# Batch 0 of a linear-attention and MLP kernel: x of two tiles made transposed and centred by TensorE, with w1 and w2 loaded in other parts

## The chip, the cores and the metric

The kernel runs on one core of a Trainium2 chip. The metric is the device time of one execution in microseconds, as the median of repeated runs. Profiles come from one profiled execution; their times count from the start of the program's span.

## The reference

```python
# batch 8, heads 8, seq 576, head_dim 64; all float32
q_s = exp(q - max) / sum          # softmax over head_dim
k_s = exp(k - max) / sum          # softmax over seq
kv  = einsum('bhsd,bhse->bhde', k_s, v)
att = einsum('bhsd,bhde->bhse', q_s, kv)
x   = att.transpose(0, 2, 1, 3).reshape(8, 576, 512)
mu, var = mean(x, -1), mean((x - mu) ** 2, -1)
xn  = (x - mu) / sqrt(var + 1e-6) * g_ln
out = x + maximum(xn @ w_ch1, 0) @ w_ch2      # 512 -> 2048 -> 512
```

## The kernel before

The 576 rows of a batch are split into 512 rows, which make a chunk of four tiles of 128, and 64 left over; the leftovers of all eight batches make a ninth chunk. The MLP of chunk 0 uses plain products. From chunk 1 on its second product, and from chunk 2 on its first product too, is done with seven block products instead of eight, from sums of blocks that VectorE and GpSimd prepare.

**Order of work.** Nothing is scheduled by a planner. `run(mlp_steps(c), side)` goes through the list of the MLP's matmuls on TensorE (PE). Each has a weight: 1 for an mm2 of 512 columns, 0.5 for 256 columns, 0.25 for 128. A side entry `(position, function)` is emitted ahead of the first matmul whose weights summed so far reach the position. In chunk 0 the first product (`mm1_part`) fills weights 0 to 64 and the second (`mm2_stream`) 64 to 128. Each engine executes its instructions in the order in which they were emitted. PE, VectorE (DVE), ScalarE (ACT), GpSimd (POOL) and the sync engine (SP) all have such an order.

**PSUM.** There are eight banks: two in the pool `att_ps` (tag `a`), six in `mm_ps` (tag `m`). A new tile of a tag takes the buffer that was taken longest ago, and waits until that one has been read.

**Start.** `first_batch` (it ends where the first `run` begins) emits batch 0 before any MLP work:
- SP loads q's first half (tiles 0 and 1) and k in four parts. POOL loads v in three parts, q's rest (tiles 2 and 3), then w1 and w2 with conversion to bf16.
- `warm(n)` is n matmuls on a tile of zeros, which nobody reads.
- `exp_qt`, `norm_q`: exp of q on ACT, then row sums, reciprocal and multiply on DVE. `eq_pT` transposes a tile by four PE transposes and copies it to `eqT`.
- `exp_k0` on ACT, `z0_mm` (column sums by PE), `recip_z`, then `kv0_mm`: 18 small matmuls for each of four pairs of heads, two pairs in one PSUM tile, and four DVE multiplies into `kv_sb`, whose blocks are diagonal.
- Tiles 0 and 1: `po_half` multiplies eqT by kv in two halves and ACT copies each half to x with a running sum; `sum_halves` adds the two sums; `xn_out` subtracts the mean on DVE; for tile 0 two pairs of PE transposes follow, each brought out by DVE with a multiply by the gain (`g_col`, the gain over 512) into `xnT`.
- Tile 1's transposes (`xn_pT`) and all of tiles 2 and 3 (`q0_rest`: sums of eqT by PE and the product; `x_fast`: scaling, sum and centring on DVE) are side entries of chunk 0.

The variance is not needed until the end of the MLP: the row's rstd scales the second product's result.

**Chunk 0's first product** takes tile 0 and tile 1 apart for the first four blocks of 128 output rows (m), 128 columns to a matmul, then both tiles together for m 4 to 7, then tiles 2 and 3 apart for m 0 to 3:

```python
parts = ((0, 2, 0, 1), (0, 2, 1, 1), (2, 2, 0, 1), (2, 2, 1, 1), (4, 4, 0, 2), (0, 4, 2, 1),
         (0, 4, 3, 1), (4, 4, 2, 2), (8, 4, 0, 2), (8, 4, 2, 2), (12, 4, 0, 2), (12, 4, 2, 2))
```

An entry is (first m, how many, first tile, how many tiles), with four contraction steps (ko) each.

**Later.** Chunk 1's attention is emitted in chunk 0's second product: `kv_all(1)` needs the leftover rows of k and v (`prep_kvrem`), which POOL loads after w1, w2, q and k.

Of the kernel before, what the change touches and what calls it, by code (L numbers as in the profile page):

```python
# [12 lines left out]
FP32 = mybir.dt.float32  # L13
# [7 lines left out]
def kernel(  # L21
# [52 lines left out]
    scrap = const.tile([P, 512], BF16)  # L74
    bones = const.tile([P, 2], BF16)
    w1_sb = wts.tile([P, KO1, DH], BF16, tag="w1", name="w1_raw")
    w1g = const.tile([P, KO1, DH], BF16)
    g_col = const.tile([P, KO1], FP32)
    ident_f = const.tile([KO1, KO1], FP32)
# [14 lines left out]
    def load_w2(g4):  # L94
        rows = slice(4 * g4, 4 * g4 + 4)
        nc.gpsimd.dma_start(w2_sb[:, rows, :], w2_src[:, rows, :])
# [187 lines left out]
    def kv0_mm(j):  # L284

        if j % 2 == 0:
            kvbox["p0"] = att_ps.tile([P, 2, 256], FP32, tag="a", name="pkv")
        pkv = kvbox["p0"]
        for t in range(T0):
            for ps in halves:  # L290
                nc.tensor.matmul(
                    pkv[ps, j % 2, 0:D], eks[0][ps, j, t], raws["v0"][ps, j, t],
                    start=(t == 0), stop=(t == T0 - 1),
                )
        if j % 2:
            for ps in halves:
                nc.vector.tensor_mul(
                    kv_sb[ps, 0, j - 1 : j + 1, ps], pkv[ps, :, 0:D],
                    kvbox["rz"][ps, j - 1 : j + 1].to_broadcast([64, 2, D]),
                )  # L300
# [45 lines left out]
    def po_mm(c, t, i):  # L346


        if i == 0:
            pool, tag = (mm_ps, "m") if c == 0 and t >= 2 else (att_ps, "a")  # L350
            pobox["p"] = pobox[c, t] = pool.tile([P, DM], FP32, tag=tag, name="po")
# [39 lines left out]
    def po_half(t, half):  # L391

        pool, tag = (mm_ps, "m") if half else (att_ps, "a")
        po = pool.tile([P, DM], FP32, tag=tag, name="po")
        for i in range(2):
            j = 2 * half + i
            nc.tensor.matmul(
                po[:, i * P : i * P + P], eqTs[0][:, t, j, :], kv_sb[:, 0, j, :],
                start=True, stop=True,
            )  # L400
        x, st, _, _ = xs[0]
        nc.scalar.activation(
            x[:, t, DH2 * half : DH2 * half + DH2], po[:, 0:DH2], AF.Copy,
            accum_out=st[:, t, half : half + 1],
        )

    def sum_halves(t):
        _, st, _, mv = xs[0]
        nc.vector.tensor_add(mv[:, t, 0:1], st[:, t, 0:1], st[:, t, 1:2])
# [120 lines left out]
    def prod(n, bank, t, k, first=False, own=False):  # L530

        at = slice(t * P, t * P + P)
        if n in (1, 2, 4):
            odd, half = ((0, 0), (1, 0), None, (1, 1))[n - 1]
            lhsT = hbox["h"][:, 2 * k + odd, 2 * half + t, :]
        else:
            lhsT = hbox["s"][:, {5: 0, 6: 1, 7: 2, 3: 3}[n], k, at]
        if n in (1, 2):
            rhs = w2_sb[:, 2 * k + n - 1, 0:DH2]
        elif n == 3:  # L540
            rhs = w2_sb[:, 2 * k + 1, DH2:DM]
        else:
            rhs = w2_q[:, {5: 0, 6: 1, 7: 2, 4: 3}[n], k]
        nc.tensor.matmul(hbox[bank][:, t], lhsT, rhs, start=first and (own or t == 0) and k == 0,  # L544
                         stop=k == KH - 1, skip_group_check=True)
# [28 lines left out]
    def last_products(product):  # L574
# [6 lines left out]

        def stt(t, col, src, add=None):
# [17 lines left out]
        def own_bank():  # L600
            bank("d")

        def seed_e():
# [15 lines left out]
        product(4, "d", ts=(1,), own=True, at={  # L619
            15: [lambda: stt(3, 0, hbox["d"][:, 1], part(3, 0)), lambda: store(3, 1, 0)]})  # L620

    def mm2_fast(c):
# [3 lines left out]
        def product(n, name, first=False, at=None, ts=range(2), own=False, cut=None):  # L626
            at = at or {}
            order = [(t, k) for t in ts for k in range(KH)]
            if cut:
                order = [(t, k) for ks in (range(cut), range(cut, KH)) for t in ts for k in ks]  # L630
            for i, (t, k) in enumerate(order):

                def go(t=t, k=k, i=i):
                    if i == 0 and first:
                        bank(name)
                    prod(n, name, t, k, first or own, own)
                    for fn in at.get(i + KH * ts[0], []):
                        fn()

                steps.append((0.5, go))  # L640
# [104 lines left out]
    def mlp_steps(c):  # L745
# [4 lines left out]
        if c == 0:  # L750
            full = range(0)
            parts = ((0, 2, 0, 1), (0, 2, 1, 1), (2, 2, 0, 1), (2, 2, 1, 1), (4, 4, 0, 2), (0, 4, 2, 1),
                     (0, 4, 3, 1), (4, 4, 2, 2), (8, 4, 0, 2), (8, 4, 2, 2), (12, 4, 0, 2), (12, 4, 2, 2))
        else:
            full, parts = range(8, KO2), ((0, 8, 0, 2), (0, 8, 2, 2))
        for m0, mn, t0, tn in parts:
# [61 lines left out]
    def second_side():  # L818
# [6 lines left out]
        s += [(9 + 2 * j, lambda j=j: cast_v(2, j)) for j in range(2)]  # L825
# [57 lines left out]
    def g_columns():  # L883
        gcp = mm_ps.tile([P, KO1], FP32, tag="m", name="gcp")
        nc.tensor.matmul(gcp, raws["g"], ident_f, start=True, stop=True)
        nc.vector.tensor_scalar_mul(out=g_col, in0=gcp, scalar1=1.0 / DM)

    def first_batch():
# [51 lines left out]
        load_w2(1)  # L940
# [11 lines left out]
        g_columns()  # L952
        exp_k0(2)
        warm(5)
        z0_mm(0)
        z0_mm(1)
        exp_k0(3)
        eq_pT(0, 1, nc.vector)
        z0_mm(2)
        warm(3)  # L960
        z0_mm(3)
        recip_z()
        for j in range(NP):
            kv0_mm(j)
        warm(2)
        po_half(0, 0)
        warm(3)
        po_half(0, 1)
        po_half(1, 0)
        po_half(1, 1)  # L970
        sum_halves(0)
        exp_qt(0, 2)
        exp_qt(0, 3)
        xn = xs[0][2]
        warm(7)
        for half in range(2):
            xn_out(0, 0, slice(DH2 * half, DH2 * half + DH2))
        for i in range(2):
            if i:
                warm(2)  # L980
            ptr = mm_ps.tile([P, 2, 2 * P], BF16, tag="m", name="ptr")
            for j in range(2):
                nc.tensor.transpose(ptr[:, j, 0:P], xn[:, 0, (2 * i + j) * P : (2 * i + j + 1) * P], ident)
            nc.vector.tensor_mul(
                xnTs[0][:, 0, 2 * i : 2 * i + 2], ptr[:, :, 0:P],
                g_col[:, 2 * i : 2 * i + 2].to_broadcast([P, 2, P]),
            )
        sum_halves(1)
        xn_out(0, 1)

# [35 lines left out]
    with tc.manual_schedule(  # L1026
# [97 lines left out]
```

## Time and profile before

| | us |
|---|---|
| median of 3 runs | 265.79 (265.69 to 265.80) |
| profiled execution | 265.6 |
| its span | 263.6 |
| PE busy | 257.4 (98%) |
| DVE busy | 217.4 (82%) |
| ACT busy | 178.8 (68%) |
| POOL busy | 76.0 (29%) |
| granted TensorE clock | 0.999 |

The span is the program's own time; 2.0 us of the execution's time lie around it. PE stands for matmuls and PEld for weight loads, which overlap them. Timeline rows give the start, the length, engine, line, operation, output and inputs, shapes, count and, in brackets, the idle time before and what ended it.

### The profile page before, as it was taken

The numbers are of one execution on the slowest core, as the hardware profiler recorded it, in microseconds if no ns is written. First come the engines' busy times: TensorE is split into PE (matmuls) and PEld (weight loads), VectorE is DVE, ScalarE is ACT, GpSimd is POOL, SyncE is SP. The second block draws the span as 40 slices with busy tenths as digits, with TensorE's granted clock in tenths as the row PEclk, the third lists the DMA queues.
The fourth block names the chain that finished last, engine by engine and source line by source line (L and its number), as shares of the span: only waits on it lengthen the run. The fifth ranks groups of instructions, "written<-read, shape, count | busy, mean of one in ns | idle before, by whom it ended". The sixth has DMA issues, their size and how long they took to land.

```text
span 263.6 us, 6818 instructions
## 1 busy us (share of the span) xinstructions
PE 257.4 (98%) x2708; PEld 218.1 (83%) x2711; DVE 217.4 (82%) x475; ACT 178.8 (68%) x350; POOL 76.0 (29%) x126
## 2 busy tenths in 40 slices
PE   8989999999999999999999999999999999999993
PEld 5778855775988998899889988998899888888882
DVE  4667797968989997989798979997999889877873
ACT  4467852896966888688868886788678377438400
POOL 8652316203049007600760076008200300030000
PEclk9999999999999999999999999999999999999999
DMA  6999999997986995799879957997804620521014
GB/s 219 256 204 208 338 208 315 271 155 233 207 151 197 325 136 97 197 308 155 93 215 298 139 99 237 297 135 146 256 6 79 161 82 12 71 90 72 0 42 119
DMA packets 69847, 45.00 MB, mean 171 GB/s; under 512 B 41460, under 2 KB 66040, under 8 KB 69816
## 3 DMA queue, kind: packets, MB, share of 16 engines
q1 hardware_dynamic: 48896, 21.76, 39.3%
q0 software_dynamic: 20320, 22.29, 38.9%
q10 hardware_dynamic: 600, 0.53, 0.6%
q8 instruction: 21, 0.34, 0.6%
q14 instruction: 10, 0.08, 0.1%
HBM read 36.70 MB, written 9.44 MB: 175 GB/s over the span
## 4 chain that ended last, share of the span: by engine, by line
PE 92%; DMA 4%; POOL 2%; issue 0%; ACT 0%; DVE 0%; POOLq 0%
PE ba L544 21%; PE bx L688 19%; PE bb L688 9%; PE ph L451 8%; PE bb L544 5%; PE be L544 5%; PE bc L544 5%; PE pc L497 5%; PE bc L688 5%; DMA w_raw<-in_moe_w_ch_dram 4%; PE ph L436 3%; PE po L353 3%; PE pkv L316 2%; PE ptr L860 1%; POOL v L931 1%; PE po L360 1%
## 5 line engine op out<-in xcount | busy, mean ns | idle before, releaser
L544 PEld LDWEIGHTS <-hs 128*128 128x128 bf16 x512 | 49.5, 98 | 5.7
L688 PEld LDWEIGHTS <-w_q 128*128 128x128 bf16 x448 | 43.1, 98 | 5.2 <-issue 0.2
L544 PEld LDWEIGHTS <-hT 128*128 128x128 bf16 x384 | 37.2, 98 | 4.4
L240 POOL TENSOR_TENSOR tq<-xnT 128x256 bf16<-128x256 bf16 x20 | 12.9, 661 | 78.6 <-DMA xnT<-xn 47.2
L688 PEld LDWEIGHTS <-w1g 128*128 128x128 bf16 x336 | 32.2, 98 | 3.9
L544 PE MATMUL ba<-w_q,hs 128*128 128x256 bf16 x256 | 31.7, 273 | 0.0
L688 PE MATMUL bx<-tq,w_q 128*128 128x256 bf16 x224 | 29.0, 273 | 0.0
L561 POOL DMA_DIRECT2D out_dram<-ot x28 | 15.3, 557 | 46.4 <-DVE ot L555 46.4
L367 ACT ACTIVATE scrap<-x,mv 128x512 bf16<-128x512 bf16 x36 | 25.9, 719 | 1.7 <-DVE x L383 1.3
L383 DVE SCALAR_TENSOR_TENSOR x<-po,rq 128x512 bf16<-128x512 f32 x34 | 23.3, 685 | 1.2 <-PE po L353 1.1
L712 ACT COPY bc<-bx 128x512 f32<-128x512 f32 x28 | 15.2, 594 | 13.0 <-PE bx L688 13.0
L719 DVE TENSOR_TENSOR bb<-bx,s 128x512 f32<-128x512 f32 x28 | 18.2, 694 | 6.3 <-ACT s L716 6.3
L730 ACT ACTIVATE hT<-bc 128x512 bf16<-128x512 f32 x28 | 15.3, 595 | 11.9 <-PE bc L688 11.9
L202 DVE TENSOR_REDUCE zq<-eq 128x16 f32<-128x1024 bf16 (+1 forms) x20 | 20.6, 1049 | 2.3 <-ACT eq L193 2.3
L528 DVE TENSOR_TENSOR hs<-hT 128x1024 bf16<-128x1024 bf16 x32 | 20.9, 674 | 0.9 <-ACT hT L730 0.5
L730 ACT ACTIVATE hT<-bb 128x512 bf16<-128x512 f32 x28 | 15.2, 595 | 8.8 <-PE bb L688 8.8
L353 PE MATMUL po<-kv_sb,eqT 128*128 128x128 bf16 x120 | 20.5, 219 | 0.0
L722 DVE TENSOR_TENSOR hT<-bx,s 128x512 bf16<-128x512 f32 x28 | 18.0, 684 | 3.0 <-PE bx L688 3.0
L569 ACT COPY s<-ba 128x512 f32<-128x512 f32 x15 | 8.7, 579 | 12.5 <-PE ba L544 7.8
L544 PE MATMUL ba<-w_sb,hT 128*128 128x256 bf16 x128 | 16.7, 273 | 0.0
L544 PE MATMUL bb<-w_q,hs 128*128 128x256 bf16 x128 | 16.6, 273 | 0.0
L497 PE MATMUL pc<-w_sb,hT 128*128 128x512 bf16 x61 | 15.6, 379 | 0.2
(135 smaller groups left out, 536.9 us busy)
## 6 DMA issues: line engine op xcount, KB each, us to landing
out_dram<-ot POOLq DMA_DIRECT2D x32, 256.0 KB, 5.9
qt<-in_q_dram SPq DMA_DIRECT2D x5, 1024.0 KB, 7.1
kt<-in_k_dram SPq DMA_DIRECT2D x5, 1024.0 KB, 15.0
vt<-in_v_dram POOLq DMA_DIRECT2D x7, 512.0 KB, 14.3
w_sb<-in_moe_w_ch_dram POOLq DMA_DIRECT2D x4, 512.0 KB, 16.1
qt<-in_q_dram POOLq DMA_DIRECT2D x2, 1024.0 KB, 14.8
kt<-in_k_dram POOLq DMA_DIRECT2D x2, 1024.0 KB, 14.3
w_raw<-in_moe_w_ch_dram POOLq DMA_DIRECT2D x3, 512.0 KB, 13.1
```

Source lines behind the costliest of these rows:

```text
L202: nc.vector.reduce_sum(eqs[c][1][:, ts], eqs[c][0][:, ts], axis=AX.X)
L353: nc.tensor.matmul(pobox["p"][:, i * P : i * P + P], eqTs[c][:, t, i, :], kv_sb[:, c, i, :], start=True, stop=True,)
L367: nc.scalar.activation(scrap, x[:, t], AF.Square, bias=mv[:, t, 0:1], scale=-float(DM), accum_out=mv[:, t, 1:2],)
L383: nc.vector.scalar_tensor_tensor(x[:, t].rearrange("p (h d) -> p h d", h=H), in0=pobox[c, t].rearrange("p (h d) -> p h d", h=H), scalar=1. ...
L451: nc.tensor.matmul(ph[:, m % 2, at : at + tn], (w1g if c else w1_sb)[:, ko, m * P : (m + 1) * P], xnTs[c][:, t0 : t0 + tn, ko, :], start=( ...
L497: nc.tensor.matmul(hbox["pc", t], hbox["h"][:, ko, t, :], w2_sb[:, ko, :], start=(ko == 0), stop=(ko == KO2 - 1),)
L528: nc.vector.tensor_tensor(out=dst, in0=x, in1=y, op=op)
L544: nc.tensor.matmul(hbox[bank][:, t], lhsT, rhs, start=first and (own or t == 0) and k == 0, stop=k == KH - 1, skip_group_check=True)
L688: nc.tensor.matmul(dst[:, q], lhsT, rhs, start=first and q == 0 and ko == 0, stop=ko == 1, skip_group_check=True)
L719: nc.vector.tensor_tensor(out=at[g, "b"], in0=at[g, "x"], in1=at[g, "s"], op=ALU.add)
L722: nc.vector.tensor_tensor(out=h_out(g, 1, 1), in0=at[g, "x"], in1=at[g, "s"], op=ALU.add)
L730: nc.scalar.activation(h_out(g, odd, half), at[g, name], AF.Relu)
```

## The change

- The kv products of batch 0 come in three groups, pairs (0, 1), (2) and (3). Each group's results go out through `kv0_out`: even heads by one DVE multiply, odd heads by ACT, then a row sum and a multiply on DVE, which write the negative mean over the 512 features as a further weight matrix (`mean_w`, in the `scrap` tile).
- For tiles 0 and 1 PE makes x already transposed and centred: `xt_mm` adds for each block j its own kv block and the four mean blocks over the 256 rows of both tiles (20 matmuls). `xt_out` brings the four blocks out with a multiply by the gain (`g_one`), two on ACT and two on DVE. x itself is still made, by `po_mm` and `x_plain`, but the MLP's start does not need it.
- ACT's exps of k all go ahead of the copies of eqT.
- w1's first 512 columns come in two halves of the contraction dimension; the first stands ahead of q's rest. The next 512 columns and the last group of w2 are each split in two.
- Chunk 0's first 16 matmuls take both tiles and go through the first two contraction steps of m 0 to 3, then the last two. The other parts and the side entries get new positions.
- `kv_all(1)` moves from weight 106 to 111, with closer entries behind it. `cast_v` of batch 2 moves from 9 and 11 to 18 and 20 in chunk 1.
- The last product of the ninth chunk is done in two halves of 128 columns with two PSUM tiles.

```diff
-        load_q0(1, nc.gpsimd)
-        load_w1(0, 256)
-        load_w1(256, 256)
-        for nb in range(1, 4):
+        for kh in range(2):
+            ks = slice(2 * kh, 2 * kh + 2)
+            nc.gpsimd.dma_start(w1_sb[:, ks, 0:512], w1_src[:, ks, 0:512])
+            if kh == 0:
+                load_q0(1, nc.gpsimd)
+        load_w1(512, 256)
+        load_w1(768, 256)
+        for nb in range(2, 4):
             load_w1(512 * nb)
...
-        warm(31)
+        warm(16)
+        g_columns()
+        warm(16)
         for t in range(2):
             exp_qt(0, t)
-        exp_k0(0)
-        exp_k0(1)
+        for j in range(NP):
+            exp_k0(j)
         norm_q(0, 0)
         norm_q(0, 1)
+        z0_mm(0)
         eq_pT(0, 0, nc.scalar)
...
+        eq_pT(0, 1, nc.scalar)
         recip_z()
-        for j in range(NP):
-            kv0_mm(j)
...
+        kv0_mm((0, 1))
+        kv0_out((0, 1))
+        warm(1)
+        kv0_mm((2,))
+        kv0_out((2,))
+        for half in range(2):
+            kvbox["xt", half] = mm_ps.tile([P, 2, 2, P], FP32, tag="m", name="xt")
+        xt_mm(0, 0, True, start=True)
+        xt_mm(1, 1, True)
+        kv0_mm((3,))
+        kv0_out((3,))
+        for i in range(NP - 1):
+            for j in range(KO1):
+                xt_mm(j, i, False, start=(i == 0 and j == 2))
+        xt_mm(2, 2, True)
+        xt_mm(3, 3, True)
+        for j in range(KO1):
+            xt_mm(j, 3, False, stop=True)
+            if j % 2:
+                xt_out(j - 1, nc.scalar)
+                xt_out(j, nc.vector)
+        for t in range(2):
+            for i in range(NP):
+                po_mm(0, t, i)
         exp_qt(0, 2)
+        x_plain(0, nc.vector)
         exp_qt(0, 3)
...
+        x_plain(1, nc.scalar)
...
+    def kv0_out(js):
+
+        pkv, rz, n = kvbox[js[0]], kvbox["rz"], len(js)
+        even, odd = halves
+        at = slice(js[0], js[0] + n)
+        nc.vector.tensor_mul(
+            kv_sb[even, 0, at, even], pkv[even, 0:n, 0:D], rz[even, at].to_broadcast([64, n, D])
+        )
+        for i, j in enumerate(js):
+            nc.scalar.mul(kv_sb[odd, 0, j, odd], pkv[odd, i, 0:D], rz[odd, j : j + 1])
+        rs = sml.tile([P, NP], FP32, tag="rs", name="rs", bufs=2)
+        nc.vector.reduce_sum(rs[:, 0:n], pkv[:, 0:n, 0:D], axis=AX.X)
+        nc.vector.scalar_tensor_tensor(
+            mean_w[:, at], in0=rs[:, 0:n].to_broadcast([P, n, P]), scalar=-1.0 / DM,
+            in1=rz[:, at].to_broadcast([P, n, P]), op0=ALU.mult, op1=ALU.mult,
+        )
+
+    def xt_mm(j, i, own, start=False, stop=False):
+
+        nc.tensor.matmul(
+            kvbox["xt", j // 2][:, j % 2], kv_sb[:, 0, i, :] if own else mean_w[:, i],
+            eqTs[0][:, 0:2, i, :], start=start, stop=stop, skip_group_check=True,
+        )
...
-            parts = ((0, 2, 0, 1), (0, 2, 1, 1), (2, 2, 0, 1), (2, 2, 1, 1), (4, 4, 0, 2), (0, 4, 2, 1),
-                     (0, 4, 3, 1), (4, 4, 2, 2), (8, 4, 0, 2), (8, 4, 2, 2), (12, 4, 0, 2), (12, 4, 2, 2))
+            parts = ((4, 2, 0, 2), (0, 4, 2, 1), (6, 2, 0, 2), (0, 4, 3, 1), (4, 4, 2, 2),
+                     (8, 4, 0, 2), (8, 4, 2, 2), (12, 4, 0, 2), (12, 4, 2, 2))
...
+            first += [
+                (0.5, lambda m=m, ko=2 * kh + ko: mm1_part(c, m, 0, 2, ko))
+                for kh in range(2) for m in range(4) for ko in range(2)
+            ]
...
-                (2, lambda: (eq_pT(0, 2, nc.scalar), xn_pT(0, 1, nc.vector), eq_pT(0, 3, nc.scalar))),
-                (2, lambda: (q0_rest(2), x_fast(0, 2))),
-                (6, lambda: q0_rest(3)),
-                (8, lambda: (xn_pT(0, 2, nc.vector), x_fast(0, 3))),
-                (16, lambda: xn_pT(0, 3, nc.vector)),
+                (4, lambda: (eq_pT(0, 2, nc.vector), eq_pT(0, 3, nc.scalar), q0_rest(2), x_fast(0, 2))),
+                (8, lambda: (q0_rest(3), xn_pT(0, 2, nc.vector), x_fast(0, 3))),
+                (18, lambda: xn_pT(0, 3, nc.vector)),
...
-            + [(106, lambda: (kv_all(1), start_x(1)))]
-            + [(111, lambda: po_x(1, 0)), (113, lambda: po_x(1, 1))]
-            + [(116, lambda: po_x(1, 2)), (118, lambda: xn_pT(1, 0, nc.scalar)), (119, lambda: square_sum(1, 0))]
-            + [(119.5, lambda: po_x(1, 3)), (123, lambda: xn_pT(1, 1, nc.scalar)), (124, lambda: square_sum(1, 1))]
+            + [(111, lambda: (kv_all(1), start_x(1)))]
+            + [(113.5, lambda: po_x(1, 0)), (115, lambda: po_x(1, 1))]
+            + [(117.5, lambda: po_x(1, 2)), (119, lambda: xn_pT(1, 0, nc.scalar)), (119.5, lambda: square_sum(1, 0))]
+            + [(120.5, lambda: po_x(1, 3)), (123, lambda: xn_pT(1, 1, nc.scalar)), (124, lambda: square_sum(1, 1))]
...
-        load_w2(2)
+        load_w2(8)
         load_behind(1, (1,))
-        load_w2(3)
+        load_w2(12, 2)
+        load_w2(14, 2)
         load_behind(2)
...
-        s += [(9 + 2 * j, lambda j=j: cast_v(2, j)) for j in range(2)]
+        s += [(18 + 2 * j, lambda j=j: cast_v(2, j)) for j in range(2)]
...
-        product(4, "d", ts=(1,), own=True, at={
-            15: [lambda: stt(3, 0, hbox["d"][:, 1], part(3, 0)), lambda: store(3, 1, 0)]})
+        product(4, "d", ts=(1,), own=True, half=0, at={15: [lambda: last_half(0)]})
+        product(4, "f", ts=(1,), own=True, half=1, at={15: [lambda: last_half(1), lambda: store(3, 1, 0)]})
```

More of the change, by code (lines that the diff above doesn't have):

```diff
@@ L78 @@
     g_col = const.tile([P, KO1], FP32)
+    g_one = const.tile([P, KO1], FP32)
     ident_f = const.tile([KO1, KO1], FP32)
@@ L282, in recip_z, with kv0_mm @@
         nc.vector.reciprocal(kvbox["rz"], kvbox["z0"][:, 0:NP])
[L284 to L300, printed above, removed]
+    def kv0_mm(js):
+        pool, tag = (mm_ps, "m") if js[0] == NP - 1 else (att_ps, "a")
+        kvbox[js[0]] = pkv = pool.tile([P, 2, 256], FP32, tag=tag, name="pkv")
+        for i, j in enumerate(js):
+            for t in range(T0):
+                for ps in halves:
+                    nc.tensor.matmul(
+                        pkv[ps, i, 0:D], eks[0][ps, j, t], raws["v0"][ps, j, t],
+                        start=(t == 0), stop=(t == T0 - 1),
+                    )
@@ new lines, in xt_mm, with xt_out @@
+    def xt_mm(j, i, own, start=False, stop=False):
+        nc.tensor.matmul(
+            kvbox["xt", j // 2][:, j % 2], kv_sb[:, 0, i, :] if own else mean_w[:, i],
+            eqTs[0][:, 0:2, i, :], start=start, stop=stop, skip_group_check=True,
+        )
+    def xt_out(j, eng):
+        src, dst, g = kvbox["xt", j // 2][:, j % 2], xnTs[0][:, 0:2, j, :], g_one[:, j : j + 1]
+        if eng is nc.scalar:
+            nc.scalar.mul(dst, src, g)
+        else:
+            nc.vector.tensor_scalar_mul(out=dst, in0=src, scalar1=g)
@@ L389, in x_fast, with x_plain @@
         xn_out(c, t)
[L391 to L399, printed above, removed]
-            )
[L401 to L409, printed above, removed]
+    def x_plain(t, eng):
+        x, _, _, mv = xs[0]
+        if eng is nc.scalar:
+            nc.scalar.activation(x[:, t], pobox[0, t], AF.Copy, accum_out=mv[:, t, 0:1])
+        else:
+            nc.vector.tensor_scalar(
+                out=x[:, t], in0=pobox[0, t], scalar1=1.0, scalar2=0.0, op0=ALU.mult, op1=ALU.add,
+                accum_out=mv[:, t, 0:1],
+            )
     def rstd_op(c):
@@ L528, in sum_h, with prod @@
         nc.vector.tensor_tensor(out=dst, in0=x, in1=y, op=op)
-    def prod(n, bank, t, k, first=False, own=False):
+    def prod(n, bank, t, k, first=False, own=False, ch=None):
         at = slice(t * P, t * P + P)
@@ L543, in prod @@
             rhs = w2_q[:, {5: 0, 6: 1, 7: 2, 4: 3}[n], k]
-        nc.tensor.matmul(hbox[bank][:, t], lhsT, rhs, start=first and (own or t == 0) and k == 0,
+        dst = hbox[bank][:, t]
+        if ch is not None:
+            cols = slice(P * ch, P * ch + P)
+            dst, rhs = dst[:, cols], rhs[:, cols]
+        nc.tensor.matmul(dst, lhsT, rhs, start=first and (own or t == 0) and k == 0,
                          stop=k == KH - 1, skip_group_check=True)
@@ L618, in last_products, with product @@
         product(4, "a", ts=(0,), at={7: [lambda: stt(2, 0, hbox["a"][:, 0]), lambda: store(2, 1, 0)]})
-        product(4, "d", ts=(1,), own=True, at={
-            15: [lambda: stt(3, 0, hbox["d"][:, 1], part(3, 0)), lambda: store(3, 1, 0)]})
+        product(4, "d", ts=(1,), own=True, half=0, at={15: [lambda: last_half(0)]})
+        product(4, "f", ts=(1,), own=True, half=1, at={15: [lambda: last_half(1), lambda: store(3, 1, 0)]})
     def mm2_fast(c):
         steps = []
-        def product(n, name, first=False, at=None, ts=range(2), own=False, cut=None):
+        def product(n, name, first=False, at=None, ts=range(2), own=False, cut=None, half=None):
             at = at or {}
@@ L635, in go @@
                         bank(name)
-                    prod(n, name, t, k, first or own, own)
+                    prod(n, name, t, k, first or own, own, half)
                     for fn in at.get(i + KH * ts[0], []):
                         fn()
-                steps.append((0.5, go))
+                steps.append((0.5 if half is None else 0.25, go))
         def seed_c():
@@ L972, in first_batch @@
         exp_qt(0, 2)
+        x_plain(0, nc.vector)
         exp_qt(0, 3)
[L974 to L987, printed above, removed]
```

38 lines of the change are left out of this document (17 added, 21 removed).

## The prediction

> **What bounds the kernel now.** I read the page first, then the chain of waits from 2 to 50 us, then the timeline of that stretch, because all edits but one lie there.
>
> ```profile
> PE 257.4 (98%) x2708; PEld 218.1 (83%) x2711; DVE 217.4 (82%) x475; ACT 178.8 (68%) x350; POOL 76.0 (29%) x126
> ...
> PE 92%; DMA 4%; POOL 2%; issue 0%; ACT 0%; DVE 0%; POOLq 0%
> ```
>
> PE is the bound almost everywhere, and after chunk 1 has begun it waits for nobody. So time won or lost on PE in chunks 0 and 1 arrives at the end unchanged, unless something takes it back before. The chain shows what comes before PE:
>
> ```profile
> 3.25 1.67 POOL v L931 x3
> 4.92 0.86 POOL qt L901
> 5.78 9.41 DMA w_raw<-in_moe_w_ch_dram
> 15.19 0.06 issue
> 15.24 0.73 PE ph L451 x8
> ```
>
> w1's first part is issued fifth on POOL, lands at 15.19, and the first MLP matmul starts at 15.24. The timeline shows that x is no earlier:
>
> ```profile
> 9.11 0.68 ACT L266 ACTIVATE ek<-kt 128x576 bf16<-128x576 f32 x1
> ...
> 10.85 1.30 PE L291 MATMUL pkv<-v,ek 64*64 64x64 bf16 x72
> ...
> 11.63 0.59 DVE L297 TENSOR_TENSOR kv_sb<-pkv,rzk 64x128 bf16<-64x128 f32 x2 [0.41 <-PE pkv L291]
> ```
> ```profile
> 14.67 0.76 DVE L984 TENSOR_TENSOR xnT<-ptr,g_col 128x256 bf16<-128x256 bf16 x2 [0.29 <-PE ptr L983]
> ...
> 16.88 0.25 PE L872 MATMUL zs<-bones,eqT 128*128 128x2 bf16 x4 [0.23 <-ACT eqT L862]
> ...
> 21.04 0.40 PE L860 MATMUL ptr<-ident,xn 128*128 128x128 bf16 x4
> ...
> 21.47 0.69 DVE L866 TENSOR_TENSOR xnT<-ptr,g_col 128x512 bf16<-128x512 bf16 x1 [0.49 <-PE ptr L860]
> ```
>
> The second half of tile 0's xnT is done at 15.43: x and w1 end together, and the change must move both. The last two rows give a number used below: from a transpose's start to the multiply's end it takes 1.12 us (21.04 to 22.16).
>
> **Part 1: when the first MLP matmul starts.** Landings, from each issue's time to landing: q's first half 5.07, k's last part 9.08, v 9.82, 10.55, 11.38, q's rest 13.08, w1's first two parts 15.19 and 15.93. In the new order w1's first half takes the place of q's rest. The three transfers move as many bytes as before, so the last still lands at about 15.9. Spacing back from there by 1.3 us for a w1 part (2.5 us for the doubly wide ones that land at 15.93, 18.44) gives q's rest at 14.6, at most 15.2 (where the old second one landed), and w1's first half at 13.3. It is then off the path.
>
> The path is the new x. exp of k's last part still ends at 9.79 (k lands at 9.08); z0's last 18 matmuls run 9.85 to 10.15, eq's second transpose follows, and kv0 starts at 10.55 instead of 10.85. A pair's product was ready for DVE 0.78 us after its start (10.85 to 11.63), so DVE starts at 11.35. Per element of a row DVE takes 1.05 ns and 0.155 us beside (0.288 at 128 wide from L297, 0.422 at 256 wide from L327). The pair then costs 0.29 (kv) + 0.29 (row sum) + 0.42 (mean weight) = 1.0, and each of the two single ones 0.22 + 0.22 + 0.29 = 0.73: the last mean weight is ready at 13.8. The trace has no row sum of 128 elements and no multiply of two broadcast operands; the ends are 0.16 and 0.42 for each, and I take the line through the two rows, which L202's 512-wide sum (0.677) also lies on. PE needs 20 matmuls of 256 columns at 0.109 = 2.2 us; with kv0's last part between them it comes to the last four at 13.98, so PE and DVE arrive together. Two results are ready at 14.35, ACT (0.38, L402) and DVE (0.42, L984) bring them out by 14.8, and the 8 plain po matmuls (0.45) fill that time. **First MLP matmul 14.85: -0.39 us.** The odd-half multiplies on ACT (0.22 each) lie beside DVE's work; the earlier gain column costs nothing while DVE waits until 5.75. Both copies of eqT now queue on ACT behind the exp that waits for k from 8.4 to 9.1; they end at 10.4 and 11.3, and eqT is read from 11.7 on.
>
> **Part 2: PE work from there to the first mm2.** Spacing in the trace is 0.0557 for 128 columns, 0.109 for 256, 0.225 for four transposes, 0.33 for zs with po. Before: 64 x 0.0557 + 96 x 0.109 + 5 x 0.225 + 2 x 0.33 = 15.81, with 0.76 of idle time, which from 15.24 gives 31.81 (seen: 31.84). After: 32 x 0.0557 + 112 x 0.109 + 4 x 0.225 + 2 x 0.33 = 15.55. **-0.26 us**, nearly all of it tile 1's transposes; joining two tiles in one matmul saves only 16 x (0.111 - 0.109). The Trainium skill ("TensorE: Matmul & The Clock Gate", Back-to-back issue gap) gives about 81 ns for a matmul of 128 columns with its weight load. By that the joining would save 0.8 us more here and part 5 would cost 0.4 more, 265.8 in all; the trace disagrees, with 55.7 ns over the rows of L451, and I give it no chance.
>
> **Part 3: new waits in chunk 0.** Both remaining eq transposes, zs and po of tile 2 stand ahead of the second half of the first 16 matmuls. ACT finishes with xT at 15.1 and then does exp of tiles 2 and 3 (0.63 each, 0.54 apart): 15.7 and 16.3. PE is done with its first 8 matmuls at 15.72; it waits 0.08 for the first exp and 0.33 for the second, and 0.19 for DVE's copy of eqT (16.3 to 16.72). The next 8 matmuls end at 17.96. Then: 0.14 for xn of tile 2; 0.25 for a PSUM buffer (the next ph takes that of the second ph, whose ReLU, behind x's copy, eqT's copy and another ReLU of 0.59 on ACT, ends at 18.85); and tile 3's transpose at weight 18 has 4 x 0.109 + 0.225 = 0.66 of PE work behind it before its result is used, against the 1.12 + 0.05 above: 0.49, where the old order had 16 matmuls between and lost 0.05. Sum 1.48 against 0.76: **+0.72 us**. First mm2: 14.85 + 15.55 + 1.48 = 31.88, against 31.84.
>
> **Part 4: chunk 1's attention, later and closer.** kv_all moves from weight 106 to 111, po of tile 0 from 111 to 113.5: between them stand 3 matmuls of 0.2165 instead of 5. DVE's reciprocal and two multiplies (42.85 to 43.93) need 1.1 us whatever stands there. Before, PE lost 0.14 in this place; now **+0.43 us**. Behind the waiting po stand mm2's matmuls and so chunk 1's start; later tiles keep up (tile 3's xn is ready 6.9 us after kv's end, PE gets there after 7.3). The move pays only if PE arrives so early that krem, landing at 41.55, would hold it; by parts 1 to 3 it doesn't.
>
> **Part 5: the last product in halves.** 16 x 0.0557 for 8 x 0.109 (+0.02), and the last DVE operation on 128 columns instead of 256 (0.48 to 0.35): **-0.11 us**.
>
> **At nothing:** two more POOL issues (0.75 each) and each later POOL transfer one place further back in the ring of eight (the ninth issue, at 10.11, waited for the first landing): hidden by a DMA backlog that lasts to 43 us. w2's third group lands at 36.96 for use at 39, the last at 43.4 for use at 44.8, and later now; if that cover went, a late w2 would cost its delay one for one. cast_v of chunk 2 goes past DVE work that nobody awaits before its kv at 58 us. Fewer warm matmuls: PE works six of the seven us before 14.85.
>
> **Sum:** -0.39 - 0.26 + 0.72 + 0.43 - 0.11 = +0.39. The profiled execution took 265.6 with a span of 263.6 (2.0 around it), 0.2 below the median; on the median it is 265.79 + 0.39 = **266.2**.
>
> **Rivals.**
> *A, faster:* the waits of part 3 are not there, because q's rest lands by 14.6 and each engine is a little quicker than added up. For it: PE's own floor is 14.85 + 15.55 = 30.4. Against it: 0.49 and 0.25 hang on engine times already measured. With 0.4 left, -1.08, so 265.1.
> *B, slower:* q's rest is late. It decides from a landing at 15.1 on, and from there each us is one on PE, since the two eq transposes stand ahead of 8 ready matmuls. At 15.93, the place of the last of the three, exp moves by 0.8: 267.0. For it: landings in one ring scatter (2.1 and 0.7 us for two equal w1 parts). Against it: the byte count.
> *C, it doesn't do what it says:* x is no earlier, because nine DVE operations take the place of four and run at the upper ends (+0.4 or so over the chain). w1 then waits and Part 1 gives 0: 266.6.
>
> **Numbers.** Forecast 0.46, with a range of its own from 265.8 to 266.5; A 0.2, B 0.24, C 0.1. A difference of 0.2%, 0.53 us, is about what a measurement of this kernel can tell from none; 266.2 lies 0.41 above. Faster is A: 0.2. Within is the forecast less the part above 266.3: 0.40. Slower is that part, B and C: 0.40. The range from 265.1 to 267.0 reaches from A to B.
>
> **What would show it.** Right: the first L451 matmul near 14.85 with w1 landed before 14; first mm2 within 0.3 of 31.9; PE waiting for ACT's eq near 16, for the ptr multiply near 21.8, for kv_out before po. Wrong: a first mm2 before 31.3 (A), eq's exp starting after 15.3 on a DMA (B), xT's first output after 14.6 (C), or PE at half pace after 8 us (0.213 apart, as the first 29 warm matmuls were).

## The result and the profile after

The changed kernel takes 267.86 us (median of 7, 266.89 to 269.09) against 265.79 (265.35 to 265.95 in as many): ratio 1.0079, 95% interval 1.0055 to 1.0103. (Ratios here and below are of mean times, so a single long execution weighs in them.) The forecast was 266.2 and the range 265.1 to 267.0, so it is slower than the range allows. Its executions also scatter over 2.2 us, those of the kernel before over 0.6. The profiled execution is the fastest of the seven: 266.89, with a span of 264.7.

The page (engines' share of the chain):

```profile
PE 257.3 (97%) x2697; PEld 217.7 (82%) x2700; DVE 217.3 (82%) x478; ACT 179.5 (68%) x350; POOL 77.4 (29%) x128
...
PE 95%; DVE 2%; ACT 1%; issue 0%
```

DMA is gone from the chain: w1's first half lands at 12.3. DVE and ACT have come in. The chain from 8 to 18 us (start, length, what) shows where:

```profile
9.18 0.38 PE z L276 x18
...
9.89 0.73 PE pkv L293 x36
...
10.64 0.29 DVE kv_sb L303
10.93 0.02 issue
10.96 0.52 ACT kv_sb L307 x2
11.47 0.02 issue
11.50 0.30 DVE rs L309
11.80 0.02 issue
11.82 0.42 DVE scrap L310
...
14.41 0.41 PE xt L317 x2
14.82 0.02 issue
14.85 0.48 ACT xnT L326
15.33 0.03 issue
15.35 0.49 DVE xnT L328
15.85 0.04 issue
15.89 0.92 PE ph L469 x7
```

ACT and DVE take turns. DVE multiplies the even heads, ACT then the odd ones, and only then does DVE sum the same PSUM tile; xT's first block goes out by ACT and its second, in the same tile, by DVE afterwards. One MLP matmul starts at 15.37, the other seven of its group at 15.89. Further on (PE's waits, total, times, longest):

```profile
...
PE po L380 <- DVE kv_sb L355: 0.4, 1, 0.4
PE ph L469 <- DVE xnT L901: 0.3, 1, 0.3
PE zs L907 <- DVE eqT L899: 0.3, 1, 0.3
PE ph L469 <- DVE xnT L328: 0.2, 1, 0.2
...
```

These are the places that the prediction named, and one more, the last. By stage, from the first matmul of each kind in the two timelines:

| us | before | after | difference |
|---|---|---|---|
| first MLP matmul, second | 15.24, 15.30 | 15.37, 15.89 | +0.13, +0.59 |
| first mm2 | 31.84 | 32.60 | +0.76 |
| chunk 1's first MLP matmul | 49.21 | 50.31 | +1.10 |
| end of the span | 263.59 | 264.66 | +1.07 |
| execution less span | 2.01 | 2.23 | +0.22 |

The remaining 1.0 us between this execution (266.89) and the median (267.86) is scatter, taken up below.

### The profile page after: what moved, and what is told of

It reads as the page before. It is cut to its first block, busy times and chain, and to the rows that moved or that the text cites. A ratio compares the mean times of both kernels' runs of the same rounds, so it can differ in the third digit from the quotient of the medians.

```text
span 264.7 us, 6800 instructions
## 1 busy us (share of the span) xinstructions
PE 257.3 (97%) x2697; PEld 217.7 (82%) x2700; DVE 217.3 (82%) x478; ACT 179.5 (68%) x350; POOL 77.4 (29%) x128
## 4 chain that ended last, share of the span: by engine, by line
PE 95%; DVE 2%; ACT 1%; issue 0%
PE ba L566 21%; PE bx L718 19%; PE bb L718 9%; PE ph L469 8%; PE bb L566 5%; PE be L566 5%; PE bc L566 5%; PE pc L515 5%; PE bc L718 5%; PE ph L454 3%; PE po L380 3%; PE warm L828 2%; PE pkv L344 2%; PE ptr L895 1%; PE z L276 1%; PE po L387 1%
## 5 line engine op out<-in xcount | busy, mean ns | idle before, releaser
L583 POOL DMA_DIRECT2D out_dram<-ot x28 | 15.3, 556 | 45.9 <-DVE ot L577 45.9
L760 ACT ACTIVATE hT<-bc 128x512 bf16<-128x512 f32 x28 | 15.3, 595 | 11.9 <-PE bc L718 11.9
L380 PE MATMUL po<-kv_sb,eqT 128*128 128x128 bf16 x128 | 21.1, 219 | 0.4 <-DVE kv_sb L355 0.4
L515 PE MATMUL pc<-w_sb,hT 128*128 128x512 bf16 x61 | 15.4, 379 | 0.3 <-issue 0.2
```

The costliest lines, as they stand in the source:

```text
L380: nc.tensor.matmul(pobox["p"][:, i * P : i * P + P], eqTs[c][:, t, i, :], kv_sb[:, c, i, :], start=True, stop=True,)
L515: nc.tensor.matmul(hbox["pc", t], hbox["h"][:, ko, t, :], w2_sb[:, ko, :], start=(ko == 0), stop=(ko == KO2 - 1),)
L760: nc.scalar.activation(h_out(g, odd, half), at[g, name], AF.Relu)
```

## The experiments

Each kernel below was run beside the kernel before; in all those runs its median was 265.4 to 265.6.

**The same two kernels again.** No edit.

> The changed kernel again, unaltered. In its first profile the full TensorE clock came at 4.7 us and the execution took 266.9, the shortest of seven (median 267.9). Theory W (clock phase): the 32 warm matmuls are a fixed number, 0.213 us each until the clock comes and 0.107 after; z0 stands behind them, so time = 266.9 + 0.5 x (clock-up - 4.7), cut off where the 32 end at 8.2 (267.9 to 268.4 for a clock-up after 7). Rival K (landing): the time follows k's last landing (8.02 in the first profile) one for one, whatever the clock does. Rival N: neither, the spread lies after the first MLP matmul.

> The changed kernel a third time, for another clock phase. W: first z0 matmul at the end of the warm ones, and the first MLP matmul as much later as z0 is. K: z0's last group and the MLP's start follow k's landing. N: MLP start within 0.2 of 15.4, and a spread after it.

> As the one before: a fourth point for clock-up, k's landing, first MLP matmul, and time. W: the four lie on one line against clock-up; K: against k's landing.

> The kernel before again. W and K: the first MLP matmul stays within 0.2 of 15.24 whatever the clock-up and k's landing are, because w1's landing at 15.2 covers both; time 265.4 to 265.9. If w1's landing itself moves with k's, the start moves with it.

Measured: 267.07, 267.00, 267.53 for the changed kernel, 265.30 for the one before. Read from the timelines, the issues' times to landing and the trace's record of the granted clock (the warm matmuls are 0.213 us apart until it rises, 0.109 after):

| | clock rises | first z0 | k's last landing | z0's end | second MLP matmul | first mm2 |
|---|---|---|---|---|---|---|
| after | 4.71 | 6.79 | 8.02 | 9.56 | 15.89 | 32.60 |
| rep_after1 | 4.48 | 6.73 | 8.44 | 9.64 | 15.97 | 32.68 |
| rep_after2 | 5.03 | 6.95 | 7.91 | 9.61 | 15.94 | 32.65 |
| rep_after3 | 5.80 | 7.27 | 8.79 | 10.00 | 16.33 | 33.21 |
| before | 7.01 | 8.75 | 9.08 | 10.99 | 15.30 | 31.84 |
| rep_before | 4.33 | 8.49 | 8.70 | 10.74 | 14.95 | 31.50 |

From z0's end to the second MLP matmul the changed kernel takes 6.33 us in all four, the old one 4.31 and 4.21. So the new way to x is 2.0 us *longer*, and what hides part of it is that z0 ends 0.7 to 1.4 earlier.

In rep_after3 z0 and all behind it came 0.4 later. Most of that is theory W: the first z0 group, which needs only k's first part (landed at 5.79), already starts 0.48 later, because the warm matmuls end later. The chain of the first 11 us in `after`, then in rep_after3 (it counts a matmul from the end of the one before, so its z0 starts 0.07 behind the timeline's):

```profile
5.01 1.85 PE warm L828 x16
6.87 0.37 PE z L276 x18
```
```profile
5.17 2.17 PE warm L828 x16
7.34 0.38 PE z L276 x18
```

W's formula gives 267.45 there, and 267.53 was measured. k's last landing adds 0.07 (from the third z0 group's end to the last one's it is 0.77 us instead of 0.70). Rival K is seen in rep_after1, where z0's last groups waited for exp of k and ended 0.09 later although the clock rose 0.23 earlier. Rival N is out: execution less z0's end is 257.3 to 257.5 us in these four profiles, and 257.4 in that of q_rest_first below, where the clock rose at 6.73 and z0 ended at 10.38. So nearly all the scatter of these profiles comes in ahead of z0's end.

The old start did move, by 0.35: there w1 landed at 13.62 and x alone held it. In all six profiles of the old start that were taken in the end, the MLP's first matmul stood either within 0.06 behind w1's landing (15.24 to 15.60, four of them) or, where w1 was early, 4.15 behind z0's end (two).

**No PSUM tile read by both engines.**

```diff
-            nc.scalar.mul(kv_sb[odd, 0, j, odd], pkv[odd, i, 0:D], rz[odd, j : j + 1])
+            pass
+        nc.vector.tensor_mul(
+            kv_sb[odd, 0, at, odd], pkv[odd, 0:n, 0:D], rz[odd, at].to_broadcast([64, n, D])
+        )
...
-            kvbox["xt", j // 2][:, j % 2], kv_sb[:, 0, i, :] if own else mean_w[:, i],
+            kvbox["xt", j % 2][:, j // 2], kv_sb[:, 0, i, :] if own else mean_w[:, i],
...
```

`xt_out` reads the blocks at their new places, and the first write of each tile has the start flag.

> The changed kernel, with nothing in batch 0's centred x read by ACT and DVE from one PSUM tile: odd heads of kv0_out go out by DVE, and xt's four blocks lie in two tiles by the engine that reads them. Theory S (shared tile): in the changed kernel DVE's row sum waits for ACT's two multiplies of the same tile (0.58 and twice 0.38), and DVE's outputs of xT wait for ACT's (the second MLP matmul at 15.89 in place of 15.48). Without that the last mean weight is ready 0.6 earlier, the eight MLP matmuls start 1.0 earlier, and the first mm2 comes 0.5 earlier (from there on exp of tiles 2 and 3, held by q's rest landing at 15.0, sets the pace): time 0.5 under the changed kernel's, some 266.5 to 267.0. Rival D: DVE's added work (0.9 us of multiplies) eats it, no change.

Measured: 267.22 (266.62 to 267.92), ratio 1.0065, interval 1.0051 to 1.0080: not told apart from the changed kernel by time. The trace tells more. The turns are gone, and z0's end to the second MLP matmul fell to 5.99, by 0.34 and not 1.0. The timeline shows what took the rest:

```profile
14.82 0.39 PE L320 MATMUL xt<-eqT,scrap 128*128 128x256 bf16 x2
15.14 0.47 ACT L329 ACTIVATE xnT<-xt,g_one 128x256 bf16<-128x256 f32 x1 [3.73 <-PE xt L320]
15.25 0.48 DVE L331 TENSOR_SCALAR xnT<-xt,g_one 128x256 bf16<-128x256 f32 x1 [0.49 <-PE xt L320]
15.66 0.39 PE L320 MATMUL xt<-eqT,scrap 128*128 128x256 bf16 x2 [0.45 <-ACT xnT L329]
```

Now PE waits to write its third block into the tile that ACT reads. So the program keeps PE's writes and a reader of one tile apart just as it does two readers; my edit exchanged one wait for the other. This profile's time, the longest of the six, says little: its clock rose at 6.88.

**kv_all back at 106** (and 111, 113, 116, 118, 119, 119.5 behind it).

> The changed kernel with chunk 1's kv_all and the entries behind it back at their old positions (106, 111, 113, 116, 118, 119, 119.5). Theory G (gap): the po of tile 0 no longer waits 0.57 for kv_out, so chunk 1 starts 0.43 earlier and the time is 0.4 lower. Rival L: kv_all now waits for the leftover k (landing 41.9, its exp 0.42), and the gain is lost: 0 or slower.

Measured: 266.91, ratio 1.0049 (1.0036 to 1.0062). From the first mm2 to chunk 1: 17.37 us, as in the kernel before; in the changed kernel 17.71. Theory G holds at 0.34, and L does not while chunk 0 is this late.

**Tile 3's transpose at weight 16.**

> The changed kernel with tile 3's transpose at weight 16 instead of 18, so that eight matmuls of 256 columns stand between it and its use, not four. Theory: PE's wait before tile 3's matmuls falls from 0.51 to 0.1, first mm2 and time 0.4 lower. Rival: at 16 xn of tile 3 isn't ready (DVE 21.4 in the first profile, PE there at 21.4), so PE waits before the transpose what it no longer waits behind it: 0 to 0.1 lower.

Measured: 267.49, ratio 1.0070 (1.0058 to 1.0082). In the trace first MLP matmul to first mm2 is 16.91 instead of 17.23: 0.32 won, as the theory says; in the time it drowns in the scatter.

**Eight warm matmuls fewer**: the second `warm(16)` becomes `warm(8)`.

> The changed kernel with 24 warm matmuls ahead of z0 instead of 32. Theory W: where the full clock comes late the 32 end after the exps of k that z0 needs, and all of batch 0 is late by that; with 24 the slow executions (268 and more) go, the spread falls from 2.2 to under 1 us and the median by 0.3 to 0.7. Where the clock comes early (4.7) nothing changes. Rival K (k's landing sets it): no change in median or spread. Rival H: with less PE work the full clock comes later or drops again, and it gets slower by up to 1 us.

Measured: 268.72 (267.02 to 270.00), ratio 1.0110 (1.0078 to 1.0143). Theory W's forecast for this edit is wrong: the spread grew. Rival H has the direction right, and some executions lost more than its 1 us. The six executions, with the mean granted clock of each, are 267.02 (0.999), 267.02 (0.999), 268.31 (0.990), 269.13 (0.985), 269.33 (0.985), 270.00 (0.979). The windows of the profiled one (length; busy time and instructions of PE, PEld, DVE, ACT, POOL; then the granted clock, the DMA share and GB/s):

```profile
8.00:10.00 2.00, 1.25 (x31) 0.73 (x29) 0.76 (x2) 1.06 (x3) 0.86 (x3) 1.00 1.20 205
10.00:12.00 2.00, 2.00 (x77) 1.64 (x77) 0.47 (x2) 1.16 (x4) 1.99 (x3) 0.96 1.18 232
12.00:14.00 2.00, 1.91 (x26) 1.27 (x25) 1.23 (x5) 0.60 (x3) 0.88 (x2) 0.50 1.11 266
14.00:16.00 2.00, 2.00 (x15) 1.55 (x14) 0.77 (x4) 0.31 (x1) 0.69 (x1) 0.69 1.39 194
```

The clock is at half from 11.8 to 15.3 us, just where PE makes xT: its matmuls of 256 columns are 0.21 apart instead of 0.109. Ahead of that, PE waited 0.75 us for exp of a k that landed at 9.18:

```profile
9.94 0.45 PE L276 MATMUL z<-ones,ek 64*64 64x1 bf16 x18 [0.75 <-ACT ek L268]
```

kv_at_106's profile (clock 0.994, k at 9.21) has the same, from 10.8 to 14.2. Of the two causes the wait for k is the larger in both: z0 ends 0.83 and 0.85 later than in `after`, and from there to the second MLP matmul it takes 6.85 and 6.68 us instead of 6.33, so the half clock costs 0.52 and 0.35.

**The warm matmuls spread out.**

```diff
         warm(16)
         g_columns()
-        warm(16)
+        warm(8)
...
+        warm(4)
         z0_mm(1)
...
-        warm(2)
+        warm(6)
         z0_mm(3)
```

> The changed kernel with 24 instead of 32 warm matmuls ahead of z0 and eight more later: 4 ahead of z0's second group, 6 in place of 2 ahead of its last, where PE waits for exp of k. Theory H (the clock drops where PE does little in a stretch of 3.41 us; seen in two traces, from 10.8 and from 11.8 us): the warm matmuls now lie in that stretch, no execution has the clock at half there (mean clock 0.997 or more in all), slowest less than 1.0 over the fastest, median 267.0. Rival K (only k's landing, 7.9 to 9.2, sets the time): spread stays as in the changed kernel, 266.9 to 269. Rival W alone (too many warm matmuls): no drop, but as with 8 fewer, where the spread rose to 3.0.

Measured: 267.92 (267.81 to 268.37 in four), ratio 1.0094 (1.0081 to 1.0107); clock 0.997 or more in all. No drop and a spread of 0.6, as H says, but not the median of 267.0: the six warm matmuls put z0's last group at 9.97 in PE's order (end 10.42), and 6.33 later, at 16.76, comes the second MLP matmul. The padding is itself on the path. Nor is H settled by four executions: the mended kernels below have the same warm matmuls, and 4 of their 43 executions show a mean clock of 0.979 to 0.987.

**q's rest first again.**

```diff
+        load_q0(1, nc.gpsimd)
         for kh in range(2):
             ks = slice(2 * kh, 2 * kh + 2)
             nc.gpsimd.dma_start(w1_sb[:, ks, 0:512], w1_src[:, ks, 0:512])
-            if kh == 0:
-                load_q0(1, nc.gpsimd)
```

> The changed kernel with q's rest ahead of w1's first half again. Theory: x, not w1, sets the MLP's start (15.4 to 16.6 in every trace of the changed kernel, w1's first half landed by 12.7), and ACT is busy with xT's output until 15.6, so q's rest at 15.0 to 15.4 holds nobody yet: w1's half lands at 14.5, no change, within 0.2. Rival B of the prediction (q's rest late): 0.4 or more faster.

Measured: 267.77, ratio 1.0084 (1.0071 to 1.0097): no gain, so rival B is not what happened. A side finding: with w1's half first, w1's second half lands at 15.9 to 16.4, with q first, here and in the mended kernels below, at 15.4.

**All mended together**: no turns on a tile and no writing behind a reader (below), kv_all at 106, the transpose at 16, warm matmuls as in warm_spread.

```diff
-        nc.vector.tensor_mul(
-            kv_sb[even, 0, at, even], pkv[even, 0:n, 0:D], rz[even, at].to_broadcast([64, n, D])
-        )
-        for i, j in enumerate(js):
-            nc.scalar.mul(kv_sb[odd, 0, j, odd], pkv[odd, i, 0:D], rz[odd, j : j + 1])
...
         nc.vector.reduce_sum(rs[:, 0:n], pkv[:, 0:n, 0:D], axis=AX.X)
...
+        for i, j in enumerate(js):
+            for ps in halves:
+                nc.scalar.mul(kv_sb[ps, 0, j, ps], pkv[ps, i, 0:D], rz[ps, j : j + 1])
...
+        for i in range(NP):
             for j in range(KO1):
...
+                xt_mm(j, i, False, start=(i == 0 and j < 2))
         for j in range(KO1):
...
+            xt_mm(j, j, True, stop=True)
+        for j in range(KO1):
+            xt_out(j, nc.vector if j % 2 else nc.scalar)
```

mended_q_first has q's rest ahead of w1's first half besides.

> All that the runs so far point to, together: row sums and mean weights by DVE first, all of kv0's multiplies by ACT behind them, xT's blocks in one PSUM tile for each engine with the outputs behind all of PE's writes; kv_all at 106; tile 3's transpose at 16; warm matmuls as in warm_spread. From z0's end to the first MLP matmul 4.75 us, against 5.81 (and 6.33 to the second) in the changed kernel and 4.2 before. Sum against the changed kernel's median 267.5: -0.9 for x, -0.34 for kv_all, -0.32 for the transpose, -0.4 for the clock: 265.5, the same as before, or 0.3 better. Rival: exp of tiles 2 and 3 now waits for q's rest (15.0 to 15.4), and 0.5 of it is lost: 266.0.

> The same with q's rest ahead of w1's first half. If q's rest is late in the mended kernel, this one is 0.3 to 0.5 faster than that (265.1 to 265.4, under the kernel before); if w1's first half (14.5) then holds the first matmul instead, no difference between the two.

Measured: 266.28 (ratio 1.0039, 1.0018 to 1.0061) and 266.13 (1.0044, 1.0017 to 1.0072). z0's end to the first MLP matmul is 4.67 us (forecast 4.75), 1.14 less than in the changed kernel, and mm2 starts at 31.80, as before the change. DVE's row sums and means no longer stop between ACT's multiplies (timeline of mended):

```profile
11.51 0.29 DVE L303 TENSOR_REDUCE rs<-pkv 128x2 f32<-128x128 f32 x1 [0.83 <-PE pkv L293]
11.84 0.42 DVE L304 SCALAR_TENSOR_TENSOR scrap<-rs,rzk 128x256 bf16<-128x256 f32 x1
11.84 2.60 ACT L310 ACTIVATE kv_sb<-pkv,rzk 64x64 bf16<-64x64 f32 x8 [0.43 <-DVE rs L303]
12.18 0.22 DVE L303 TENSOR_REDUCE rs<-pkv 128x1 f32<-128x64 f32 x1
```

The rival's place was wrong. What took back 0.5 lies further on: from the first mm2 to chunk 1 it is 17.87 us instead of 17.37, mostly because kv_all at 106 now waits for DVE's cast of v of batch 1 (`vm`):

```profile
42.28 0.87 PE L341 MATMUL pkv<-vm,ek 128*64 128x65 bf16 x32 [0.36 <-DVE vm L136]
```

v itself had landed at 40.47; DVE comes to the cast only at 41.58. It has worked without a pause since the row sums of batch 1's q, 34.30 to 41.58, just as in the kernel before from 33.98 to 41.24; q of batch 1 landed 0.59 later (32.24 against 31.65), and the two casts took 0.89 instead of 0.76. In mended_q_first DVE was only 0.09 later, but one cast took 0.72 instead of 0.42. Both long casts overlap with POOL's issuing of a load of k (41.02 to 41.91, and 40.93 to 41.82); that this made them long is not shown.

Three of their 19 executions took 268.6 to 269.9, with the clock at 0.979 to 0.987.

**kv_all at 108**, po at 113, on mended_q_first; then the same with the old tail.

> mended_q_first with kv_all at 108 and po of tile 0 at 113, so five matmuls between them but both two later. In mended_q_first kv_all waited about 0.4 for cast_v, whose v lands 0.6 later than in the kernel before. Theory: that wait goes and nothing comes for it: 0.35 lower, 265.7 to 265.8. Rival: po and the transposes behind it are now too close to chunk 1 and the 0.35 is lost there: 266.1.

> mended_q_108 with the last product of the kernel before, whole. E: outside the span 2.0 again, time 0.15 to 0.23 lower, 265.75. M: outside the span still 2.23, time 0.0 to 0.1 higher than 265.96. In neither case under the kernel before (265.44): the new x, mended, starts the MLP no earlier than the old.

Measured: 265.96 (1.0026, 1.0010 to 1.0042) and 266.15 (1.0023, 1.0006 to 1.0041). From first mm2 to chunk 1 it takes 17.27 to 17.30, so the wait is gone. Its reason was not the one expected, a late v: v landed over 1 us ahead of its cast here (40.07 and 40.09, casts from 41.46 and 41.48), and 0.9 ahead in mended_q_first (40.38, 41.33). Of the 24 executions four took 267.4 to 267.8 at a full clock (two of each kernel), and one 269.75 with the clock at 0.979; no profile shows what the four waited for. mended_q_108 is the best version found, and the kernel before is still faster.

**Parts of the change alone on the kernel before.** kv_all and its followers at the new places; w1's first 256 columns ahead of q's rest; the last product in halves; and, not part of the change, without `warm(3)` between z0's last groups.

> The kernel before with only kv_all(1) and the entries behind it at the new positions (111, 113.5, 115, 117.5, 119, 119.5, 120.5). Theory G: three matmuls in place of five stand between kv and po, PE waits 0.34 to 0.43 more there and nothing takes it back: 265.5 + 0.35 to 0.4 = 265.9. Rival: PE is early enough here that the later place saves a wait for the leftover k: no change or faster.

> The kernel before with only w1's first 256 columns ahead of q's rest. Theory X (x sets the MLP's start): w1 lands at 13 and the first MLP matmul still follows k's last landing by 6.2; q's rest lands at 15 and exp of tile 2 starts then, 0.7 later than before, which holds eq's transposes by 0.1 to 0.3: 265.5 to 265.8. Rival B' (w1's landing sets the start, as the chain of waits of the first profile says): 0.1 to 0.5 faster. Rival T: the whole POOL stream is 0.5 later (seen in every trace with w1 ahead of q), v of batch 1 with it, and kv_all waits 0.3 for it.

> The kernel before with only the last product in two halves of 128 columns. In all twelve kernels' profiles that have this tail with the new start, 2.23 us of the execution lie outside the span; in the five with the old kernel's start and tail 1.97 to 2.02. Theory E (the tail's end): the halves bring that 0.23, and 265.44 becomes 265.55 to 265.7 with nothing gained inside the span. The prediction's term: 0.11 faster, 265.33. Rival M: the 0.23 belongs to the start (two more transfers, other code), and here the execution less its span stays 2.0.

> The kernel before without the three warm matmuls between z0's last two groups. Theory: PE's own order, not k, holds z0's last group (10.54, with exp done at 9.79); without them kv0 and the whole of x come 0.43 earlier and the start follows until w1's landing (13.6 to 15.2) holds it: 0.2 to 0.4 faster, 265.1 to 265.3. Rival H: with less PE work the clock drops for 3.41 us in some executions: those 1 to 3 us slower.

Measured, against 265.44 to 265.46:

| | median | ratio, interval |
|---|---|---|
| before_kv_111 | 265.78 | 1.0013, 1.0004 to 1.0021 |
| before_w1_ahead | 265.72 | 1.0010, 1.0001 to 1.0018 |
| before_tail_halves | 265.46 | 1.0000, 0.9990 to 1.0009 |
| before_no_warm3 | 265.76 | 1.0013, 1.0002 to 1.0023 |

kv_all's new place costs 0.34 alone. In its timeline po waits for kv_out where nothing else is late:

```profile
45.22 0.38 PE L353 MATMUL po<-kv_sb,eqT 128*128 128x128 bf16 x4 [0.41 <-DVE kv_sb L327]
```

w1 ahead of q's rest gains nothing alone: it lands at 12.07, and the start, 15.04, is 4.15 behind z0's end (theory X). Its executions spread by 0.64 only (265.48 to 266.12), although w1 holds nothing there. The halves are worth nothing, and execution less span stays 2.0 with them, 2.23 in the last mended kernel without them. So the 0.23 does not come from the tail, and before_kv_111 (1.97) and before_w1_ahead (1.98) don't have it either: it stays with the rest of the change. Without the warm matmuls z0 ends at 10.30, but in that profile w1 landed at 15.55 and the start came at 15.60; some executions gain 0.2 (265.24), others lose 1.0 (266.5, one with the clock at 0.991).

## Why the prediction was wrong

- **What bounds the kernel:** right. x and w1 end within 0.1 of each other in the old start, and either alone can hold it.
- **Part 1 is the step that failed** (-0.39; first MLP matmul 14.85). DVE's single durations were right: row sums 0.29 and 0.23 (forecast 0.29 and 0.22), mean weights 0.42 and 0.29 (the same), kv multiplies 0.28 and 0.21; ACT's multiplies took 0.31 instead of 0.22. Its sentence that the odd multiplies on ACT lie beside DVE's work was wrong, and so was bringing xT out on both engines at once. In turns a pair took 1.60 (10.64 to 12.24) instead of 1.0, a single one 1.05 to 1.13 instead of 0.73, and the outputs 1.35 (14.85 to 16.2) instead of 0.45. From z0's end that is 6.33 us to the second MLP matmul. The forecast's own times give 4.7 (z0's last group from 9.85, with the 0.44 that it takes in the trace, and the second matmul 0.11 behind 14.85); mended, it was 4.9. The Trainium skill ("PSUM — Partial Sum Buffer", PSUM bank collisions raise a hardware error) says that any two engines must be kept apart on a PSUM bank, two readers included, where their partitions overlap. The trace shows this program doing so: DVE's row sum over 128 partitions waits 0.58 for ACT's multiplies on 64 of them. That ACT also waits for DVE's multiply of the other half of the partitions is the program's own wait, by whole tiles. I should have weighed that page against this step.
- **Part 2** (-0.26) and **Part 3** (+0.72) together forecast +0.46 from the MLP's start to mm2. Counted from the second matmul it was 16.71 against 16.54, so +0.17, where the forecast, counted so, gives +0.38. Waits: 0.46 at zs, 0.22 at tile 2's transpose, 0.51 at tile 3's; 1.3 in all without the new one, forecast 1.48. That the sums are near is in part luck: the 0.41 for the exps did not appear, because PE came to them 0.93 later than forecast (16.65 for 15.72) and they ended only 0.4 to 0.5 later, and the copy of eqT cost 0.46 in place of 0.19. Tile 3's term was right, and xn3_at_16 gave 0.32 of it back.
- **Part 4:** right; +0.43 forecast, +0.34 in the trace and alone.
- **Part 5:** -0.11 forecast, 0 measured. DVE's last operation did take 0.35 instead of 0.48, and in before_tail_halves it ended 0.08 earlier, counted from chunk 1's start; but from there to the span's end it was 3.74 us instead of 3.66.
- **At nothing:** the later POOL transfers cost nothing in the changed kernel. The clock and k's landing, put at nothing, were not: z0 now stands right behind the 32 warm matmuls and follows the clock's rise (3.95 to 6.88) and k's landing (7.9 to 9.2), and ends at 9.56 to 10.46. In the old order it doesn't: in the five profiles of the old start that keep `warm(3)`, z0 ends at 10.74 to 10.99 while the clock rises anywhere from 3.8 to 7.0.
- **Rivals:** A was out. B's landing came true (q's rest at 14.92 to 15.39 in the four profiles of the changed kernel), but ACT was busy with xT until 15.57 in the first of them anyway, and q_rest_first gained nothing. C had the right effect, x no earlier, with the wrong cause and size: it put the start back by 0.39, and the second matmul came 0.93 behind the forecast's 14.96 in the fastest profile, although k landed 1.06 earlier there than in the profile before.
- **The sum:** for the profiled execution the forecast was 265.6 + 0.39 = 266.0, and 266.89 was measured. Of these 0.9 the start makes +0.93, the stretch to mm2 -0.21, Part 4 -0.09, Part 5 +0.1, and the time outside the span, in no case of the prediction, +0.22. Between this execution and the median lies the scatter, 1.0 against 0.2 in the kernel before, in no case of the prediction either.

**Open:** what the 0.23 is. And the scatter of the unprofiled executions is not split: a clock that rises late is shown in rep_after3, no_shared_psum and q_rest_first (the last two have their first z0 at 7.80 and 7.73, although k's parts had landed as early as in the others), a late k with a clock that drops in two profiles; how often each occurs otherwise was not tried.

## To carry to other kernels

When work that one engine did is divided between two, look for a PSUM tile that both touch: then they take turns, and the division adds their times instead of hiding one. Before moving work ahead in an engine's order, ask what its late place has been absorbing: here z0, once it stood right behind the warm matmuls, followed k's landing and the clock's rise, which the old order hid. A side entry moved later needs as much work between it and its consumer as before.

## What the runs showed of the hardware

The clock can fall without a long idle stretch of PE. In the two profiles with a drop it fell 6.83 us after it had risen and came back 3.41 us later. PE's longest wait between that rise and that fall was 0.75 us (0.73 in kv_at_106), and much of its work was matmuls of one column and 64 columns. warm_spread has the same small matmuls, a wait of 0.61 us ahead of z0, and no drop; what decides is not shown. In the eight profiles with 32 warm matmuls ahead of z0 the full clock came between 3.95 and 6.88 us, and the first z0 matmul from 6.7 to 7.8.
